# Routed attention and a gated feed-forward on one core: row sums of the first four groups by TensorE in place of GpSimd, their division one turn sooner, weight rounding from turn 0

## The chip, the cores and the metric

The kernel runs on one core of one Trainium2 chip. The metric is the time of one execution in microseconds (us) on the device; the median of 7 runs is given. TensorE (PE) multiplies; its weight loads (PEld) overlap the products. VectorE (DVE), ScalarE (ACT) and GpSimd (POOL) work on whole tiles, each engine in the order in which its instructions were issued. SyncE (SP) issues nearly all DMAs, in order too.

## What is computed

```python
# q, k, v: (4, 8, 768, 64); centroids: (8, 16, 64); all fp32
q_assign = argmax(q_n @ c_n.T)              # nearest of 16 centroids, per head
k_assign = argmax(k_n @ c_n.T)
mask   = q_assign[:, :, :, None] == k_assign[:, :, None, :]
scores = where(mask, q @ k.T / 8, -1e9)
attn   = softmax(scores)                    # along the keys
x      = (attn @ v), heads side by side     # (3072, 512)
h      = x @ w_in                           # (512, 2048)
out    = (h * sigmoid(1.702 * h)) @ w_out   # (2048, 512)
```

`w_in` and `w_out` arrive as 64-bit floats and are rounded to fp32 on the chip.

## The kernel before

**Units, groups, turns.** Two heads make a pair `p` (16 pairs, four per batch; `HP` is 4). A group `g` is one pair with one half (384) of its queries; the first four groups (g below `HP`) are the first half of the first batch, the next four its second half. A group has six units, one per tile of 128 keys (`kt` 0 to 5). Scores are held transposed: 128 keys on the partitions, 384 queries of each of the two heads along the free dimension. The main loop (L551 on) takes two units per turn, so a group lasts three turns (`TG`), a batch 24 (`TB`), and there are 96 turns and two more to drain.

**One turn, in the order issued.** `scores` (L384, PE) writes two PSUM tiles `s` of a pool with two buffers. In the first batch `part` (L398, PE) adds a product of one-hot codes to them, which makes pairs of query and key with different centroids hugely negative; `exps` (L409, ACT) takes the exponential. In later batches the mask is a multiplication on DVE instead (L420). `mask` also adds up the row sums: for each unit with `kt` above 0 POOL adds the 128x768 tile `A` into `sum` (L430), five adds per group. `values` (L441, PE) handles the units of the turn before: for each of the two heads one product of 64 columns of `v` with `A`, accumulated over the six units in a PSUM tile `o`; after the last unit ACT copies `o` to `x` (L446).

**Division.** `normalise(g)` runs in turn 3g+4. It multiplies `sum` by a tile of ones (L453, PE, two products), which adds up the 128 partitions and spreads the result over 64 rows; DVE takes the reciprocal (L456) and multiplies `x` by it (L458). In the first half of the first batch it stands behind the turn's preparation, later ahead of it. `check` (L468, L470, ACT) then takes statistics of the reciprocal.

**Preparation of pairs.** `PREP` has seven steps: four `prep_turn` (three transposes on PE, L262, then a copy on ACT, L267), `prep_near` (products with the centroids, L276, copy L282), `prep_assign` (transposes L287, then four or five DVE instructions, L293 to L308, which find the nearest centroid) and `prep_hot` (twelve transposes, L349, evacuated by DVE, L354, and ACT, L356), or for later pairs `prep_spread`. All these, the products of the division and the feed-forward part share PSUM tiles from one pool, `ps_m`, with three buffers (`bank()`). `prep(p, 0)` loads `v` of its pair, and steps 1 and 3 load the next `q` or `k`. Assignments of the pairs 1 to 4 fall in the turns 1, 3, 6 and 9, `prep_hot` of pairs 1 to 3 in the turns 2, 4 and 7.

**Weights.** 32 chunks of 128x512, 512 KB each as read. `load_w` issues a DMA on SP into one of three `raw` buffers. `split_w` has two DVE instructions (L159, L161), then two on ACT (L163, L165); `join_w` three on DVE (L171, L174, L177). `round_next` loads chunk i+2, splits chunk i and joins chunk i-1, which frees the buffer that the load needs. Before, it is called once in the turns 1, 2, 4, 5, 6, 8, 9 and 10, and from turn 12 on two or three times per turn. The feed-forward part calls `round_to` to force what it needs.

**Feed-forward.** After every fourth group `normalise` appends 28 pieces: 16 of `first` (four products of `w_in` with `x`, L487, tanh on ACT, L492, gate on DVE, L494) and 12 of `second` (four products each with `w_out`, L504). `rate` spreads them over the turns: `owed` grows by it in every turn that begins with pieces left. The pieces stand at the end of a turn.

Of the kernel before, what the change touches and what calls it, by code (L numbers as in the profile page):

```python
# [38 lines left out]
def fast(  # L39
# [21 lines left out]
    nc = tc.nc  # L61

    B, H, S, D = q.shape
# [3 lines left out]
    NJ = S // P  # L67
    HALF = S // 2
    NH = NJ // 2
    HP = H // 2  # L70
    NPAIR = B * HP
    NCH = DM // P
    NF = DF // P
# [24 lines left out]
    def bank():  # L98
        return ps_m.tile([P, 512], FP32, name="m")

    def short():
        return tmp.tile([P, HALF], FP32, name="short")
# [4 lines left out]
    def load_qk(p, w):  # L107
        t = inp.tile([P, NJ, 2, D], FP32, name="in")
        b, hp = divmod(p, HP)
        for a in range(2):  # L110
            nc.sync.dma_start(
                out=t[:, :, a, :],
                in_=(q, k)[w][b, 2 * hp + a].rearrange("(p j) d -> p j d",
                                                       j=NJ))
        qk_in[p, w] = t

    def load_v(p):
        b, hp = divmod(p, HP)
        t = pairs.tile([P, 2, NJ, D], FP32, name="inv")
        nc.sync.dma_start(  # L120
            out=t.rearrange("p a j d -> p a (j d)"),
            in_=v[b, 2 * hp:2 * hp + 2].rearrange(
                "a (p j) d -> p a (j d)", j=NJ))
        v_in[p] = t
# [18 lines left out]
    def load_w(i):  # L143
        if i < NW:
            t = wp.tile([P, WN, 2], I32, name="raw")
            nc.sync.dma_start(out=t.rearrange("p n t -> p (n t)"),
                              in_=w_chunks[i][1])
            w_raw[i] = t
# [5 lines left out]
    def split_w(i):  # L154

        hi = w_raw[i][:, :, 1]
        w = w_chunks[i][0]
        e = wp.tile([P, WN], I32, name="e")
        nc.vector.tensor_scalar(out=e, in0=hi, scalar1=EXP, scalar2=None,  # L159
                                op0=ALU.bitwise_and)  # L160
        nc.vector.tensor_scalar(out=w.bitcast(I32), in0=hi, scalar1=0xFFFFF,  # L161
                                scalar2=None, op0=ALU.bitwise_and)
        nc.scalar.activation(out=e, in_=e, func=AF.Relu, scale=8.0,  # L163
                             bias=low[:, 0:1])
        nc.scalar.activation(out=w, in_=w.bitcast(I32), func=AF.Copy,  # L165
                             scale=2.0 ** -20, bias=1.0)
        w_pow[i] = e

    def join_w(i):
        raw, e, w = w_raw.pop(i), w_pow.pop(i), w_chunks[i][0]  # L170
        nc.vector.scalar_tensor_tensor(  # L171
            out=e, in0=raw[:, :, 1], scalar=-2 ** 31, in1=e,
            op0=ALU.bitwise_and, op1=ALU.bitwise_or)
        nc.vector.scalar_tensor_tensor(  # L174
            out=w, in0=raw.bitcast(U32)[:, :, 0], scalar=2.0 ** -52, in1=w,
            op0=ALU.mult, op1=ALU.add)
        nc.vector.tensor_tensor(out=w, in0=w, in1=e.bitcast(FP32),  # L177
                                op=ALU.mult)
# [3 lines left out]
    def round_next():  # L182
        i = w_done[0]
        if i < NW:
            load_w(i + 2)
            split_w(i)
        if 0 < i <= NW:
            join_w(i - 1)
        w_done[0] += 1

    def round_to(n):
        while w_done[0] <= min(n, NW):
            round_next()

    load_qk(1, 0)
    load_v(0)


# [10 lines left out]
    ones = const.tile([P, D], FP32, name="ones")  # L209
# [34 lines left out]
    for a in range(2):  # L244
        rows = slice(a * D, (a + 1) * D)
        nc.vector.tensor_copy(
            out=cT[rows, :, a, :],
# [120 lines left out]

    NG = 2 * NPAIR
    NU = NG * NJ  # L370
    s_of, A_of, sum_of, o_of, O_of, xT_of = {}, {}, {}, {}, {}, {}

    def split(g):
        b, r = divmod(g, 2 * HP)
        h, hp = divmod(r, HP)
        return b * HP + hp, h

    def scores(u):
        g, kt = divmod(u, NJ)
        p, h = split(g)  # L380
        ps = ps_s.tile([P, 2, 512], FP32, name="s")
        for a in range(2):
            rows = slice(a * D, (a + 1) * D)
            nc.tensor.matmul(out=ps[:, a, 0:HALF],  # L384
                             lhsT=T[p, 1][rows, kt * P:(kt + 1) * P],
                             rhs=T[p, 0][rows, h * HALF:(h + 1) * HALF],
                             start=True, stop=(p >= HP))
        s_of[u] = ps[:, :, 0:HALF]
# [22 lines left out]

    def mask(u):

        g, kt = divmod(u, NJ)
        p, h = split(g)
        s = s_of.pop(u)
        if p >= HP:
            A_of[u] = ap.tile([P, 2, HALF], FP32, name="A")
            for a in range(2):
                nc.vector.scalar_tensor_tensor(  # L420
                    out=A_of[u][:, a, :],
                    in0=qcode[p][:, a, h * HALF:(h + 1) * HALF],
                    scalar=code[p][:, kt % NH, 1, kt // NH, a:a + 1],
                    in1=s[:, a, :], op0=ALU.is_equal, op1=ALU.mult)
        A = A_of[u]
        if kt == 0:
            return
        if kt == 1:
            sum_of[g] = ap.tile([P, 2, HALF], FP32, name="sum", bufs=2)
        nc.gpsimd.tensor_tensor(out=sum_of[g],  # L430
                                in0=A_of[u - 1] if kt == 1 else sum_of[g],
                                in1=A, op=ALU.add)

    def values(u):
        g, kt = divmod(u, NJ)
        p, h = split(g)
        if kt == 0:
            o_of[g] = ps_o.tile([P, 512], FP32, name="o")
        A = A_of.pop(u)
        for a in range(2):  # L440
            nc.tensor.matmul(out=o_of[g][a * D:(a + 1) * D, 0:HALF],  # L441
                             lhsT=v_in[p][:, a, kt, :], rhs=A[:, a, :],
                             start=(kt == 0), stop=(kt == NJ - 1))
        if kt == NJ - 1:
            O_of[g] = xp.tile([P, HALF], FP32, name="x")
            nc.scalar.copy(O_of[g], o_of.pop(g)[:, 0:HALF])  # L446

    def normalise(g):

        sm = sum_of.pop(g)  # L450
        ps = bank()
        for a in range(2):
            nc.tensor.matmul(out=ps[a * D:(a + 1) * D, 0:HALF], lhsT=ones,  # L453
                             rhs=sm[:, a, :], start=True, stop=True)
        rec = recs[g] = short()
        nc.vector.reciprocal(out=rec, in_=ps[:, 0:HALF])  # L456
        x = xT_of[g] = O_of.pop(g)
        nc.vector.tensor_tensor(out=x, in0=x, in1=rec, op=ALU.mult)  # L458
        if g % HP == HP - 1:
            ffn.extend(ffn_chunks(g // HP))  # L460
# [14 lines left out]
    ffn = deque()  # L475
# [47 lines left out]
    TG = NJ // 2  # L523
    TB = 2 * HP * TG

    prep_at = {}
    for p in range(1, NPAIR):
        b, hp = divmod(p, HP)
        for i in range(2 if p == 1 else 0, len(PREP)):
            if p == 1:  # L530
                t = (i - 2) // 2
            elif b == 0:
                t = (hp - 2) * TG + 1 + i // 2
            else:
                t = b * TB + (-20, -8, -2, 1)[hp] + i
# [5 lines left out]
    def prep(p, i):  # L541
        if i == 0 and p:
            load_v(p)
        PREP[i](p)
        if i in (1, 3) and loads:
            load_qk(*loads.popleft())

    rate = (NF + NH * (NF // 4)) / (TB / 2 - 0.5)
    owed = 0.0
    for p, i in [(0, i) for i in range(6)] + [(1, i) for i in range(2)]:  # L550
        prep(p, i)  # L551
        if p == 0 and i in (1, 3):
            load_w(i // 2)
    for t in range(NT + 2):
        us = range(2 * t, 2 * t + 2) if t < NT else ()
        for u in us:
            scores(u)
        if t == 0:
            prep(0, 6)
        for u in us:  # L560
            part(u)
        for u in us:
            exps(u)
        second = t >= TB // 2
        if second:
            round_next()
        for u in us:
            mask(u)
        work = sorted(prep_at.get(t, ()), key=lambda w: PREP[w[1]] != prep_near)
        while work and PREP[work[0][1]] == prep_near:  # L570
            prep(*work.pop(0))
        if 1 <= t <= NT:
            for u in range(2 * t - 2, 2 * t):
                values(u)
        owed = owed + rate if ffn else 0.0
        g = (t - 2) // TG if t >= 2 and (t - 2) % TG == TG - 1 else None
        if g is not None and second:
            normalise(g)
        for p, i in work:
            prep(p, i)  # L580
        if g is not None and not second:
            normalise(g)
        if recs:
            check(*recs)
        if second or t and t % 4 != 3:
            round_next()
        while owed >= 1 and ffn:
            ffn.popleft()()
            owed -= 1
        if second and t % 2:  # L590
            round_next()


    ok = const.tile([P, 2, 2 * NPAIR], FP32, name="ok")
# [6 lines left out]
    ps = bank()  # L601
# [451 lines left out]
```

## Time and profile before

| what | value |
|---|---|
| median of 7 runs | 1088.79 us |
| lowest and highest | 1086.58 and 1089.24 us |
| the profiled execution's own time | 1086.99 us |
| its span, first to last instruction | 1085.2 us |
| mean granted TensorE clock | 0.989 |
| POOL L430, 160 adds | 294.2 us busy, 1839 ns each |
| first score product; first `w_in` product | 11.80 us; 93.65 us |

The page of the profile gives each engine's busy time and share, then the span in 40 slices of 27.1 us, one digit each: the busy share in tenths, and for PEclk the clock that was granted. A row of the stretches gives the limits and the length of the stretch, then for PE, PEld, DVE, ACT and POOL the busy us with the number of instructions, the granted clock, the share of the DMA engines and GB/s. A row of a timeline gives the start, the length (from the first start to the last end), engine, line, operation, output, inputs, shapes and count, and in brackets the idle time of the engine before it with what ended it. An fp32 product appears as two records on PE, so a turn's four `values` products are eight records.

### The profile page before, as it was taken

The numbers are of one execution on the slowest core, as the hardware profiler recorded it, in microseconds if no ns is written. First come the engines' busy times: TensorE is split into PE (matmuls) and PEld (weight loads), VectorE is DVE, ScalarE is ACT, GpSimd is POOL, SyncE is SP. The second block draws the span as 40 slices with busy tenths as digits, with TensorE's granted clock in tenths as the row PEclk, the third lists the DMA queues.
The fourth block names the chain that finished last, engine by engine and source line by source line (L and its number), as shares of the span: only waits on it lengthen the run. The fifth ranks groups of instructions, "written<-read, shape, count | busy, mean of one in ns | idle before, by whom it ended". The sixth has DMA issues, their size and how long they took to land. (4 is left out here: it accounts for less than half of the span.)

```text
span 1085.2 us, 10456 instructions
## 1 busy us (share of the span) xinstructions
PE 1048.2 (97%) x3982; PEld 492.7 (45%) x3982; DVE 491.2 (45%) x744; ACT 354.5 (33%) x665; POOL 295.4 (27%) x168
## 2 busy tenths in 40 slices
PE   7878799999999999999999999999999999999997
PEld 4323354445544455445554455444554445444543
DVE  3889999135442444424453164423552244431200
ACT  4664555233322333223432233223332133311100
POOL 2654232213222333122231142222232333230000
PEclk9998899999999999999999999999999999999999
DMA  8533453111100010102200000010000000000000
GB/s 216 149 95 102 132 148 94 47 49 26 41 22 27 10 30 15 31 25 54 51 23 17 20 16 15 15 56 24 8 9 10 10 10 1 1 10 20 1 11 22
DMA packets 64812, 45.13 MB, mean 42 GB/s; under 512 B 51952, under 2 KB 57584, under 8 KB 64752
## 3 DMA queue, kind: packets, MB, share of 16 engines
q1 hardware_dynamic: 64608, 44.33, 14.3%
q8 instruction: 33, 0.54, 0.2%
q14 instruction: 27, 0.22, 0.1%
q10 hardware_dynamic: 144, 0.03, 0.0%
HBM read 38.04 MB, written 6.31 MB: 41 GB/s over the span
## 5 line engine op out<-in xcount | busy, mean ns | idle before, releaser
L430 POOL TENSOR_TENSOR sum<-sum,A 128x768 f32<-128x768 f32 x128 | 235.4, 1839 | 460.6 <-DVE A L420 364.2
L487 PE MATMUL m<-x,w_in 128*128 128x384 f32 x1024 | 348.4, 495 | 10.0 <-ACT T L267 4.4
L504 PE MATMUL m<-w_out,g 128*128 128x512 f32 x768 | 337.8, 594 | 0.7 <-ACT short L282 0.7
L420 DVE SCALAR_TENSOR_TENSOR A<-qb,code,s 128x384 f32<-128x384 uint8 x288 | 157.6, 610 | 274.7 <-ACT s L409 251.9
L487 PEld LDWEIGHTS m<-x,w_in 128*128 128x128 f32 x1024 | 193.0, 193 | 150.5 <-issue 18.2
L504 PEld LDWEIGHTS m<-w_out,g 128*128 128x128 f32 x768 | 143.3, 190 | 175.6 <-issue 171.5
L494 DVE SCALAR_TENSOR_TENSOR g<-g,m 128x384 f32<-128x384 f32 x128 | 70.0, 553 | 219.8 <-ACT g L492 219.8
L384 PE MATMUL s<-T,T 64*128 64x384 f32 x768 | 151.5, 513 | 8.2 <-ACT A L409 8.2
L409 ACT ACTIVATE s<-s 128x768 f32<-128x768 f32 x144 | 107.9, 793 | 136.1 <-PE s L384 136.1
L441 PE MATMUL o<-A,inv 128*64 128x384 f32 x768 | 145.8, 501 | 0.0
L492 ACT ACTIVATE g<-m 128x384 f32<-128x384 f32 x128 | 61.5, 486 | 196.1 <-PE m L487 195.9
L430 POOL TENSOR_TENSOR sum<-A 128x768 f32<-128x768 f32 x32 | 58.8, 1838 | 215.6 <-DVE A L420 179.5
L384 PEld LDWEIGHTS s<-T,T 64*128 64x128 f32 x768 | 66.0, 187 | 91.6 <-issue 51.4
L456 DVE RECIPROCAL short<-m 128x384 f32<-128x384 f32 x32 | 81.7, 2552 | 25.8 <-PE m L453 25.8
L441 PEld LDWEIGHTS o<-A,inv 128*64 128x64 f32 x768 | 46.8, 137 | 84.7 <-issue 84.4
L510 ACT ACTIVATE y<-m 128x512 f32<-128x512 f32 x24 | 14.3, 594 | 155.9 <-PE m L504 142.7
L468 ACT ACTIVATE short<-short 128x384 f32<-128x384 f32 x32 | 16.7, 523 | 109.5 <-DVE x L458 109.5
L409 ACT ACTIVATE A<-s 128x768 f32<-128x768 f32 x48 | 36.1, 804 | 20.2 <-PE s L398 20.2
L267 ACT COPY T<-m 128x384 f32<-128x384 f32 x64 | 29.7, 479 | 37.0 <-PE m L262 36.9
L262 PE MATMUL m<-ident,in 128*128 128x128 f32 x192 | 33.7, 296 | 3.0 <-ACT T L267 1.7
L163 ACT ACTIVATE e<-e,low 128x512 int32<-128x512 int32 x32 | 23.1, 723 | 30.8 <-DVE e L159 30.6
L262 PEld LDWEIGHTS m<-ident,in 128*128 128x128 f32 x192 | 21.4, 146 | 22.1 <-issue 11.1
(68 smaller groups left out, 373.9 us busy)
## 6 DMA issues: line engine op xcount, KB each, us to landing
raw<-in_moe_w_in_dram SPq DMA_DIRECT2D x16, 512.0 KB
raw<-in_moe_w_out_dram SPq DMA_DIRECT2D x16, 512.0 KB
in<-in_q_dram SPq DMA_DIRECT2D x32, 192.0 KB
in<-in_k_dram SPq DMA_DIRECT2D x32, 192.0 KB
inv<-in_v_dram SPq DMA_DIRECT2D x16, 384.0 KB
out_dram<-y SPq DMA_DIRECT2D x24, 256.0 KB
qb<-line SPq DMA_DIRECT2D x12, 192.0 KB
line<-row SPq DMA_DIRECT2D x12, 1.5 KB
```

Source lines behind the costliest of these rows:

```text
L262: nc.tensor.transpose(out=ps[:, n * P:(n + 1) * P], in_=qk_in[p, w][:, h * NH + n].rearrange("p a d -> p (a d)"), identity=ident)
L267: nc.scalar.copy(dst, ps[:, 0:HALF])
L384: nc.tensor.matmul(out=ps[:, a, 0:HALF], lhsT=T[p, 1][rows, kt * P:(kt + 1) * P], rhs=T[p, 0][rows, h * HALF:(h + 1) * HALF], start=True, ...
L409: nc.scalar.activation(out=A_of[u] if p < HP else s, in_=s, func=AF.Exp, scale=SCALE)
L420: nc.vector.scalar_tensor_tensor(out=A_of[u][:, a, :], in0=qcode[p][:, a, h * HALF:(h + 1) * HALF], scalar=code[p][:, kt % NH, 1, kt // NH ...
L430: nc.gpsimd.tensor_tensor(out=sum_of[g], in0=A_of[u - 1] if kt == 1 else sum_of[g], in1=A, op=ALU.add)
L441: nc.tensor.matmul(out=o_of[g][a * D:(a + 1) * D, 0:HALF], lhsT=v_in[p][:, a, kt, :], rhs=A[:, a, :], start=(kt == 0), stop=(kt == NJ - 1))
L456: nc.vector.reciprocal(out=rec, in_=ps[:, 0:HALF])
L487: nc.tensor.matmul(out=ps[:, 0:HALF], lhsT=w_in[:, c, f * P:(f + 1) * P], rhs=xT[c], start=(c == 0), stop=(c == NCH - 1))
L492: nc.scalar.activation(out=g, in_=ps[:, 0:HALF], func=AF.Tanh, scale=0.851)
L494: nc.vector.scalar_tensor_tensor(out=g, in0=g, scalar=1.0, in1=ps[:, 0:HALF], op0=ALU.add, op1=ALU.mult)
L504: nc.tensor.matmul(out=ps[:, 0:DM], lhsT=hs[f][:, n * P:(n + 1) * P], rhs=w_out[:, f, :], start=(f == 0), stop=(f == NF - 1))
```

## The change

For the first four groups the row sums come from PE: next to each `values` product stands one of `ones` with the same `A`, accumulated over the six units in a PSUM tile `D_of[g]` taken from `ps_m` at the group's first unit. POOL adds nothing for these groups, and `normalise` reads `D_of[g]` directly, without products of its own. Their division comes in turn 3g+3 instead of 3g+4, ahead of the turn's preparation. The first two weight loads are issued before and after the load of pair 1's `q`; one `round_next` stands ahead of the assignment of pair 0, one in the middle of turn 0, and one at the end of every turn; from turn 12 on there are two per turn. The feed-forward pieces of the first half are spread over one turn more.

```diff
+    load_w(0)
     load_qk(1, 0)
+    load_w(1)
     load_v(0)
...
     def mask(u):
...
-        if kt == 0:
+        if kt == 0 or g < HP:
             return
...
     def values(u):
...
+        if g < HP:
+            if kt == 0:
+                D_of[g] = bank()
+            for a in range(2):
+                nc.tensor.matmul(out=D_of[g][a * D:(a + 1) * D, 0:HALF],
+                                 lhsT=ones, rhs=A[:, a, :], start=(kt == 0),
+                                 stop=(kt == NJ - 1))
...
     def normalise(g):
-        sm = sum_of.pop(g)
-        ps = bank()
-        for a in range(2):
-            nc.tensor.matmul(out=ps[a * D:(a + 1) * D, 0:HALF], lhsT=ones,
-                             rhs=sm[:, a, :], start=True, stop=True)
+        if g < HP:
+            ps = D_of.pop(g)
+        else:
+            sm = sum_of.pop(g)
+            ps = bank()
+            for a in range(2):
+                nc.tensor.matmul(out=ps[a * D:(a + 1) * D, 0:HALF], lhsT=ones,
+                                 rhs=sm[:, a, :], start=True, stop=True)
...
-    rate = (NF + NH * (NF // 4)) / (TB / 2 - 0.5)
+    norm_at = {TG * g + (TG if g < HP else TG + 1): g for g in range(NG)}
     owed = 0.0
     for p, i in [(0, i) for i in range(6)] + [(1, i) for i in range(2)]:
+        if (p, i) == (0, 5):
+            round_next()
         prep(p, i)
-        if p == 0 and i in (1, 3):
-            load_w(i // 2)
...
         second = t >= TB // 2
-        if second:
+        if second or t == 0:
             round_next()
...
-        owed = owed + rate if ffn else 0.0
-        g = (t - 2) // TG if t >= 2 and (t - 2) % TG == TG - 1 else None
-        if g is not None and second:
-            normalise(g)
+        if not ffn:
+            owed = 0.0
+        else:
+            owed += (NF + NH * (NF // 4)) / (TB / 2 - 0.5 + (t < TB + 1))
+        if t in norm_at:
+            normalise(norm_at[t])
         for p, i in work:
             prep(p, i)
-        if g is not None and not second:
-            normalise(g)
         if recs:
             check(*recs)
-        if second or t and t % 4 != 3:
-            round_next()
+        round_next()
         while owed >= 1 and ffn:
             ffn.popleft()()
             owed -= 1
-        if second and t % 2:
-            round_next()
```

More of the change, by code (lines that the diff above doesn't have):

```diff
@@ L370, in fast @@
     NU = NG * NJ
-    s_of, A_of, sum_of, o_of, O_of, xT_of = {}, {}, {}, {}, {}, {}
+    s_of, A_of, sum_of, o_of, D_of, O_of, xT_of = {}, {}, {}, {}, {}, {}, {}
     def split(g):
```

## The prediction

> **What bounds the kernel now.** I read the busy shares first, then the 40 slices, then stretches of the span, then the timelines of the engines.
>
> ```profile
> span 1085.2 us, 10456 instructions
> PE 1048.2 (97%) x3982; PEld 492.7 (45%) x3982; DVE 491.2 (45%) x744; ACT 354.5 (33%) x665; POOL 295.4 (27%) x168
> ...
> PE   7878799999999999999999999999999999999997
> ...
> DVE  3889999135442444424453164423552244431200
> ...
> PEclk9998899999999999999999999999999999999999
> ```
>
> Over the whole span PE is the bound. Only its first five slices (136 us) are below nine tenths, and there DVE has nines and the granted clock eights. So whatever the change gains must come out of that stretch, and any PE work it adds is paid in full unless it falls into a hole there. The same stretch cut at the start of turn 0, of turn 12 and of turn 17:
>
> ```profile
> 11.80:80.44 68.64, 56.34 (x380) 24.73 (x380) 50.97 (x75) 42.21 (x80) 34.92 (x18) 0.99 0.51 141
> 80.44:136.31 55.87, 46.15 (x168) 20.97 (x168) 54.85 (x69) 28.67 (x52) 19.67 (x10) 0.83 0.39 120
> 136.31:200.00 63.69, 62.67 (x259) 29.56 (x259) 55.60 (x83) 33.41 (x63) 19.01 (x10) 1.00 0.36 108
> ```
>
> After the length come PE, PEld, DVE, ACT and POOL busy, then the clock. PE is idle for 68.64 - 56.34 = 12.3 us in turns 0 to 11 and 55.87 - 46.15 = 9.7 us in turns 12 to 16. In the second stretch the clock of 0.83 costs another 46.15 x 0.17 = 7.8 us. Together 29.8 us can be won back; from turn 17 on PE is full (1.0 us idle). In turns 12 to 16 DVE is busy 54.85 of 55.87 us: DVE is the bound there, and POOL is part of the reason:
>
> ```profile
> 80.53 4.39 POOL L430 TENSOR_TENSOR sum<-sum,A 128x768 f32<-128x768 f32 x2 [3.77 <-ACT A L409]
> ```
> ```profile
> 78.37 0.68 DVE L174 SCALAR_TENSOR_TENSOR w_in<-raw,w_in 128x512 f32<-128x512 uint32 x1
> ...
> 80.96 2.29 DVE L174 SCALAR_TENSOR_TENSOR w_in<-raw,w_in 128x512 f32<-128x512 uint32 x1
> 83.29 2.18 DVE L177 TENSOR_TENSOR w_in<-w_in,e 128x512 f32<-128x512 f32 x1
> ```
> ```profile
> 74.93 1.51 PE L441 MATMUL o<-A,inv 128*64 128x384 f32 x8
> 80.44 2.93 PE L384 MATMUL s<-T,T 64*128 64x384 f32 x8 [4.00 <-ACT A L409]
> ```
>
> The same L174 takes 0.68 us alone and 2.29 us while POOL adds: one of the rounding's instructions is held about 1.6 us per add. PE then waits 4.00 us for the exponentials, which stand on ACT behind the rounding's L163 and L165, and those behind DVE. After the hole L384 takes 2.93 us instead of 1.56: the clock had been halved.
>
> **The change, part by part.**
>
> *Products with ones.* Each of the 24 units of groups 0 to 3 gets two products of the form of L441 (128x64 weights, 384 columns, the two halves of PE's columns in turn). A turn of L441 goes from 41.35 to the next start at 42.80 us, 1.45 us. Twelve turns cost 12 x 1.45 = 17.4 us. The four L453 pairs that go took 0.75 each (120.49 to 121.24), 3.0 us. PE has **14.4 us more to do**. If the added products interleave worse than L441, the bound above is a full-array product like L487 (2.65 us per 8 records, 17.4 x 2.65/1.45 = 31.8 us); below, nothing for a product that falls into a hole. I take 17.4, since shape and alternation are L441's.
>
> *POOL's additions.* Twenty adds of 1.84 us leave. POOL itself bounds nothing. What is saved is about ten holdups on DVE in turns 1 to 13 at 1.6 us, 16 us of DVE; a clean round is 2.60 us (42.69 to 45.29). From turn 12 the second half's adds go on as before, five per three turns.
>
> *Rounding sooner.* Before, 8 rounds are done by the end of turn 11; now 1 ahead of the first assignment, 2 in turn 0, 1 in each of turns 1 to 11: 14. Six rounds, 15.6 us of DVE, leave turns 12 to 21, where two per turn replace two or three. Each round also puts L163 and L165 (0.62 + 0.52 us) on ACT ahead of the next exponentials.
>
> *Loads.* SP issues raw 0 and 1 ahead of pair 1's q and of v 0. At 229 GB/s (the first 20 us) 512 KB take 2.3 us, so q of pair 1 lands 2.3 us later, v 0 and k of pair 1 4.6 us later. Their first uses are at 11.06, 19.79 and 16.21 us, and they were issued at 3.51, 5.23 and 6.39: covered, 0. Uncovered, up to 2.3 us. Later raw loads wait on SP for a round's join, with q and k loads behind them; those run more than two turns ahead. 0.
>
> *Division sooner, and a bank held.* The division of group g moves from turn 3g+4, after that turn's preparation, to turn 3g+3, before it. There it stands on DVE ahead of the assignment (turns 3, 6, 9), which the round follows. The row sums hold one of the three PSUM banks for three turns, so the preparation has two. Let E be the end of the products in turn 3. DVE then does L456 and L458 (2.67 + 0.47 us), five assignment instructions (2.73), split (0.67), join (1.93), then L354 (0.56): bank free at E + 9.1. PE meanwhile has L287 0.4, scores and masks 1.91, values and ones 2.9, a 0.6 wait for the assignment, transposes 0.76: it stands at E + 6.6 and waits for a bank. Two more banks through ACT's L356 and L267 bring the next scores to E + 10.75, against E + 7.4 unblocked: **3.4 us lost in turn 4**. In turn 7, with one transpose group instead of three behind it, the same sum gives 2.7. In turn 10 the way runs over ACT: 3.14 + 2.73 + L159 0.45 + L163 0.62 + L165 0.52 + first exponential 0.85 = E + 8.3, against 5.3 of PE work: 2.9. Turn 0 keeps its 0.67 + 0.90, and turns 1 and 2 lose 1.6 to bank and ACT waits. Turns 0 to 12: **12.2 us**, no less than the 12.3 before, only at other places.
>
> *Turns 13 to 17.* The feed-forward part starts in turn 13 instead of 14, and x of group 3 (division at E + 3.2) arrives before its first product (E + 3.35), so the 2.81 us wait at 98.66 goes. DVE per turn has two rounds 5.2, adds' holdups 5/3 x 1.6 = 2.7, 2.24 gates x 0.5 = 1.1, division 1.0: 10.0 us. PE has 3.35 + 2.24 x 2.65 + 0.5 = 9.8. Nearly even, so short bank waits stay: 0.7 in turn 15, 3.4 in turn 16, 0.6 in turn 17 (the same place as the 4.14 us wait at 128.51). **4.7 us**. Bounds: 0 if DVE keeps ahead, 9.7 as before.
>
> *Sum.* 14.4 + 12.2 + 4.7 - 29.8 = **+1.5 us** on the profiled execution (1086.99 us, 1.8 over its span). The median is 1.8 above that execution, so 1088.79 + 1.5 = 1090.3 us. Break-even is a loss of 15.4 us where I find 16.9.
>
> *The clock.* Holes of 2.77 us and more halved it, the hole of 2.05 us at 46.05 did not, nor did the 3.5 us between 54.85 and 58.32 that hold only transposes and 1.36 us of waiting. My holes are 2.1 to 2.4 us, and transposes stand beside them, so I charge nothing. One drop costs 1.6 to 2.5 us.
>
> The Trainium skill (TensorE: Matmul & The Clock Gate, Part 4: PE-mode transpose) says that transposes do not count as busy for the clock in the way products do, and its Part 1 gives a window of about 3.4 us. The stretch from 54.85 speaks against taking that literally. By the page, turn 4 (5.5 us with transposes alone) and turn 7 (3.8 us) would each drop the clock, and the sum would be some 4 us higher, an estimate.
>
> **Rivals.**
>
> *DVE freed, holes filled.* DVE's 16 us of holdups and six early rounds leave so much slack that turns 13 to 17 lose nothing and the division turns only half of what I charge: 14.4 + 7.7 - 29.8 = -7.7 us, 1081. For it: DVE's 54.85 of 55.87. Against: in turns 3, 6 and 9 the chain is one of order, not of load.
>
> *The clock falls in the division turns.* Holes in turns 4, 7 and 10 grow past about 2.8 us, as at 98.66, and PE runs at half speed after each: 3 x 2.0 on top, +7.5 us, 1096. It decides once DVE's L354 comes later than E + 9.5. For it: holes within 0.5 us of that size. Against: the stretch from 54.85.
>
> *No effect of the adds' absence.* If DVE's long instructions had another cause than POOL, turns 1 to 11 would still be held up; the chain of turn 3 would grow by 1.6, towards 1095. The coincidence of each 2 us instruction with an add speaks against it.
>
> **How the numbers follow.** Near even, 1086 to 1094: 0.45. Freed, below 1086: 0.33. Clock or longer chain, above 1094: 0.22. The predicted time is 1090. A measurement here tells 0.2%, 2.2 us, from no change; of the near-even case 0.27 lie inside and 0.18 above, so faster 0.33, same 0.27, slower 0.40. As both signs weigh, the near-even case's own range is 1086 to 1094; the range that leaves two in ten out is 1080 to 1096.
>
> **What would show it.** Added products near 0.72 us per unit; no DVE rounding over 0.7 us before turn 12; PE waits of 2 us in turns 4, 7 and 10, named by DVE's L354 or ACT's exponentials; first w_in product near 101 us; clock 1.0 up to there. A start of w_in below 96 us makes me wrong on the fast side; a clock below 0.95 before turn 12 on the slow side.

## The result, and the profile after

The changed kernel takes 1091.77 us (median of 13 runs, 1090.15 to 1094.05); the kernel before, run beside it, 1088.68 us. The ratio is 1.0034 with a 95% interval of 1.0026 to 1.0041: slower by 0.3%, 3.1 us by the medians. The prediction was 1090 us, in a range of 1080 to 1096. The profiled execution took 1092.73 us, 5.7 us above the one of before. That is more than the medians differ by, since the first stood 1.0 above its median and the second 1.7 below the 1088.68 of before; the stages below add up to the difference of the spans, 5.6 us.

The page of the changed kernel, the lines that answer to those of before (busy time and share, then tenths of 40 slices):

```profile
span 1090.8 us, 10566 instructions
PE 1059.3 (97%) x4062; PEld 497.3 (46%) x4062; DVE 477.2 (44%) x744; ACT 355.6 (33%) x665; POOL 257.5 (24%) x148
...
PE   7888989999999999999999999999999999999997
...
DVE  4757999124443354414453163423552344431200
```

POOL has lost its 20 adds (37.9 us) and DVE 14.0 us with the same 744 instructions: that is the time for which the adds had held it up. PE has 80 records more (96 for the products with ones, less the 16 of the four divisions). Apart from the last slice, still five slices are below nine tenths, and the sum of the first six has hardly risen (46 before, 48 after).

The stretches of the changed kernel, cut at the start of turns 0, 12, 17 and 22 (limits, length, busy PE, PEld, DVE, ACT and POOL, clock, DMA share, GB/s):

```profile
13.18:96.75 83.57, 73.03 (x457) 31.82 (x456) 55.33 (x97) 50.00 (x89) 0.00 (x0) 0.96 0.48 139
96.75:144.67 47.92, 41.84 (x182) 19.09 (x180) 42.78 (x56) 23.00 (x42) 15.54 (x8) 1.00 0.40 124
144.67:200.41 55.74, 54.98 (x221) 25.86 (x220) 44.76 (x67) 26.93 (x52) 16.25 (x8) 1.00 0.29 88
```

| stage | before | after | difference |
|---|---|---|---|
| up to turn 0 | 11.80 us | 13.18 us | +1.4 |
| turns 0 to 11 | 68.64 us, PE idle 12.3, clock 0.99 | 83.57 us, idle 10.5, clock 0.96 | +14.9 |
| turns 12 to 16 | 55.87 us, idle 9.7, clock 0.83 | 47.92 us, idle 6.1, clock 1.00 | -8.0 |
| from turn 17 on | 948.9 us | 946.1 us | -2.8 |

By the start of turn 17 the changed kernel has one feed-forward piece more behind it, 2.65 us, which the last row gives back. So turns 12 to 16 give 10.6 us and turns 0 to 11 take 14.9. In the first stretch PE waits almost as long as before, at other places. PE's timeline in turn 4, from the last products with ones to the scores of turn 5, and at the end of turn 7:

```profile
43.16 0.81 PE L451 MATMUL m<-A,ones 128*64 128x384 f32 x4
44.80 0.86 PE L351 MATMUL m<-ident_h,hot 128*64 128x128 bf16 x12 [0.83 <-DVE hot L310]
47.87 1.84 PE L264 MATMUL m<-ident,in 128*128 128x128 f32 x9 [2.21 <-DVE qb L356]
49.64 2.93 PE L386 MATMUL s<-T,T 64*128 64x384 f32 x8
...
71.95 0.55 PE L264 MATMUL m<-ident,in 128*128 128x128 f32 x3 [2.34 <-DVE qb L356]
72.43 2.31 PE L386 MATMUL s<-T,T 64*128 64x384 f32 x8
```

The bracket names the instruction whose end let PE go on: DVE's copy out of the bank that the next transposes need. After both holes the scores take 2.93 and 2.31 us instead of 1.56: the clock was halved (granted clock 0.50 from 49.64 to 52.51 us and 0.61 from 72.43 to 75.42). And DVE's and SP's timelines around turn 12:

```profile
102.46 0.43 DVE L159 TENSOR_SCALAR e<-raw 128x512 int32<-128x512 int32 x1 [4.69 <-DMA raw<-in_moe_w_in_dram]
```
```profile
92.85 0.38 SPq L332 DMA_DIRECT2D line<-row  x1
96.63 0.34 SPq L334 DMA_DIRECT2D qb<-line  x1
97.06 0.85 SPq L146 DMA_DIRECT2D raw<-in_moe_w_in_dram  x2
```

SP issued pair 4's `line` at 92.85, stood until it had landed to issue `qb` from it at 96.63, and only then issued weight chunk 14. DVE idled 4.69 us for it, and the division of group 3, on which the feed-forward part waits, stands behind it.

### The profile page after: what moved, and what is told of

It is laid out like the page before. It is cut to its first block, busy times and chain, and to the rows that moved or that the text cites. A ratio compares the mean times of both kernels' runs of the same rounds, so it can differ in the third digit from the quotient of the medians.

```text
span 1090.8 us, 10566 instructions
## 1 busy us (share of the span) xinstructions
PE 1059.3 (97%) x4062; PEld 497.3 (46%) x4062; DVE 477.2 (44%) x744; ACT 355.6 (33%) x665; POOL 257.5 (24%) x148
## 5 line engine op out<-in xcount | busy, mean ns | idle before, releaser
L500 PE MATMUL m<-x,w_in 128*128 128x384 f32 x1024 | 343.3, 489 | 5.0 <-DVE g L507 2.7
L433 POOL TENSOR_TENSOR sum<-sum,A 128x768 f32<-128x768 f32 x112 | 204.8, 1828 | 425.2 <-DVE A L423 361.9
L500 PEld LDWEIGHTS m<-x,w_in 128*128 128x128 f32 x1024 | 190.1, 190 | 143.5 <-issue 12.3
L433 POOL TENSOR_TENSOR sum<-A 128x768 f32<-128x768 f32 x28 | 51.3, 1834 | 294.4 <-DVE A L423 177.9
```

What stands on the lines that cost most here:

```text
L433: nc.gpsimd.tensor_tensor(out=sum_of[g], in0=A_of[u - 1] if kt == 1 else sum_of[g], in1=A, op=ALU.add)
L500: nc.tensor.matmul(out=ps[:, 0:HALF], lhsT=w_in[:, c, f * P:(f + 1) * P], rhs=xT[c], start=(c == 0), stop=(c == NCH - 1))
```

## The experiments

Times are medians. Each ratio is taken against runs of the kernel before on the same chip (1087.6 to 1088.1 us).

**Row sums back on POOL, earlier rounding kept (a_pool_sums).**

```diff
-        if kt == 0 or g < HP:
+        if kt == 0:
...
-        if g < HP:
+        if g < 0:
...
-    norm_at = {TG * g + (TG if g < HP else TG + 1): g for g in range(NG)}
+    norm_at = {TG * g + (TG + 1): g for g in range(NG)}
...
```

The lines left out put the division of these groups behind the preparation again and the pieces back to their old pace.

> Row sums of groups 0 to 3 back on POOL and their division back in turn 3g+4 behind the preparation; only the earlier rounding and loads of the change stay. Theory: the products with ones are the cost (14.4 us of PE) and the earlier rounding alone is a gain in turns 12 to 16, partly paid back in turns 0 to 11, where DVE goes from 51 busy of 68.6 us to about 67 and is still held up by adds. Expected 1086 us (1083 to 1090), with DVE instructions of 2.2 us back before turn 12. Rival (the earlier rounding and loads are what costs, the sums are neutral): 1091 us or more.

1089.39 us, ratio 1.0011 (1.0002 to 1.0020): between the two, and the expected gain isn't there. DVE is held up in turns 1 to 12 as before (an L174 of 2.32 us at 52.13, of 2.31 at 71.00, of 2.30 at 88.76), now with six more rounds to do, and PE has waits of 1.86, 1.37, 1.38, 2.38 and 3.99 us up to the start of turn 12, for DVE's copies or for exponentials. The earlier rounding alone moves the shortage forward, it doesn't remove it. By the ratio it costs 1.2 us (0.2 to 2.2), so it isn't all of the 3.1 us either.

**Row sums on PE, rounding and loads as before (b_sums_alone).**

```diff
-    load_w(0)
...
-        round_next()
+        if second or t and t % 4 != 3:
+            round_next()
...
+        if second and t % 2:
+            round_next()
```

> Products with ones and the earlier division stay; rounding and loads are as in the kernel before (8 rounds by the end of turn 11, none in turns 3 and 7). Theory: 15.6 us of DVE come back into turns 12 to 21, where DVE is the bound, while turn 4 loses less because no round stands in turn 3. Expected 1095 us (1091 to 1100), DVE full in turns 12 to 16 with clock drops there. Rival (the rounding's place is worth nothing): 1091.8 us, within 1 us.

1096.97 us, ratio 1.0077 (1.0061 to 1.0094), as expected: with the sums on PE the kernel is 9 us above the one before without the earlier rounding, and 3 with it. Here turn 3 happens to have no round, and the 2.21 us wait of turn 4 is 0.31 us. Turn 6 has one, and the wait of turn 7 is the same 2.34 us as in the changed kernel, but this time the scores behind it run at full clock:

```profile
66.47 0.55 PE L262 MATMUL m<-ident,in 128*128 128x128 f32 x3 [2.34 <-DVE qb L354]
66.94 1.56 PE L384 MATMUL s<-T,T 64*128 64x384 f32 x8
```

**No rounding in the division turns (c_round_off).**

```diff
-        round_next()
+        for _ in range(1 if second or t in (0, 11) else t % TG):
+            round_next()
```

> As the changed kernel, but no rounding in turns 3, 6 and 9 (two rounds in turns 2, 5 and 8 instead), so that the copy that frees a bank and the exponentials no longer stand behind split and join. Theory (the holes of turns 4, 7 and 10 are an order of instructions on DVE, 2.6 us too late, and bring the clock down): the waits of 2.2, 2.3 and 2.1 us fall below 1 us, the clock stays at 1.0 before turn 12, expected 1085 us (1082 to 1088). Rival (the holes come from DVE's load or from the held bank alone): 1091 us, within 1.5 us.

1081.22 us, ratio 0.9931 (0.9919 to 0.9943): 10.5 us below the changed kernel with the same instructions in another order, and 3.8 us below what I had expected. The same places on PE's timeline:

```profile
44.45 0.86 PE L351 MATMUL m<-ident_h,hot 128*64 128x128 bf16 x12 [0.82 <-DVE hot L310]
45.62 1.66 PE L264 MATMUL m<-ident,in 128*128 128x128 f32 x9 [0.31 <-DVE qb L356]
47.21 1.56 PE L386 MATMUL s<-T,T 64*128 64x384 f32 x8
...
66.09 0.55 PE L264 MATMUL m<-ident,in 128*128 128x128 f32 x3 [0.32 <-DVE qb L356]
```

The waits of 2.21 and 2.34 us are 0.31 and 0.32, the third, 2.08 us in turn 10, is gone, and the scores run at full clock. The bank is still held and DVE has the same load: what made the holes was that the copy and the exponentials stood behind split and join.

**Few products with ones (g_few_ones), and the same without rounding in the division turns (h_round_off_few_ones).**

```diff
             if kt == 0:
                 D_of[g] = bank()
-            for a in range(2):
+            for a in range(2 if kt in (0, NJ - 1) else 0):
```

> As the changed kernel, but products with ones only for the first and the last key tile of each of groups 0 to 3 (16 of 24 units' products left out, so the row sums of these groups are incomplete); the bank is held as long, DVE and ACT do the same. Prices the products: theory says they lie on PE's path, 16 x 0.72 = 11.6 us, expected 1080 us (1078 to 1084). Rival (they fall into PE's holes): 1088 us or more.

> No rounding in turns 3, 6 and 9, and products with ones only for the first and last key tile of each of groups 0 to 3 (the row sums of these groups are incomplete). Prices the products once the holes are gone. Theory (16 of 24 units' products came to 5.5 us instead of 11.6 with the holes there, because a hole that is a chain from the end of the sums grew as PE came sooner, and the clock fell three times): now 8 to 11.6 us below the version with all products (1081.2), 1071 us (1069 to 1074). Rival (half of the products' time is hidden whatever the holes): 1076 us or more.

The first took 1086.22 us, ratio 0.9987 (0.9977 to 0.9997), 5.5 us below the changed kernel; the second 1076.44 us, ratio 0.9904 (0.9889 to 0.9919), 4.8 us below c_round_off. I had expected 11.6 and then 8 to 11.6. By the ratios, each against the kernel before on its own chip, it is 5.1 and 2.9 us. So leaving a product out gives back roughly a quarter to a half of its time on PE, with the holes or without; the expectation's reason for the first miss can't be the whole one, since it doesn't hold for the second. PE's timeline of h_round_off_few_ones shows where some 3 us of the rest go:

```profile
40.43 0.86 PE L351 MATMUL m<-ident_h,hot 128*64 128x128 bf16 x12 [1.26 <-DVE hot L310]
54.34 0.55 PE L289 MATMUL m<-ident,short 128*128 128x128 f32 x3 [1.34 <-ACT short L284]
75.91 0.22 PE L325 MATMUL m<-ident_h,qc 128*12 128x128 bf16 x1 [1.68 <-DVE qc L318]
```

In turns 4 and 10 PE comes sooner to what DVE's division and assignment have to deliver (0.82 and 0.44 us in c_round_off), and in turn 6 it waits 1.34 us for ACT where it didn't. A product that fills such a wait costs next to nothing.

**qb's load a turn later (e_line_first), and both orders mended (j_round_off_line).**

```diff
+        def spread():
+            nc.sync.dma_start(
...
+        late.append(spread)
+        if p > HP:
+            late.pop()()
...
         round_next()
+        if t == 11:
+            late.pop()()
```

> As the changed kernel, but the second of pair 4's two small loads (qb from line, which stands on SP until line has landed) is issued at the end of turn 11 instead of turn 10, so that the load of weight chunk 14 no longer stands behind it. Theory (the wait of 4.7 us of DVE for that chunk at 102 us is SP's order, and costs PE about 1.7 us in turn 13 and part of the bank waits of turns 14 to 16): the wait falls below 2.5 us, expected 1089.5 us (1088 to 1091). Rival (the wait is the transfer itself, or DVE has slack there): 1091.8 us, within 1 us.

> Both orders mended: no rounding in turns 3, 6 and 9, and qb's load of pair 4 one turn later on SP. Theory: 1 to 2 us below the version with the first alone (1081.2): 1079.5 us (1078 to 1081). Rival (the chunk's wait is hidden): 1081 us, within 0.7 us.

e_line_first: 1090.63 us, ratio 1.0024 (1.0013 to 1.0036). The interval overlaps that of the changed kernel, so the time alone doesn't decide. The waits of its DVE between 80 and 140 us do:

```profile
DVE e L159 <- DMA raw<-in_moe_w_in_dram: 0.7, 2, 0.4
```

The columns are total, times and longest: 0.7 us instead of 4.7. PE's waits of 1.19 us (turn 13) and 1.76 us (turn 14) are gone with it. j_round_off_line: 1079.69 us, ratio 0.9930 (0.9917 to 0.9944), within its expectation; against c_round_off 1.5 us less by the medians, but only 0.1 by the ratios, with overlapping intervals again. That the wait was SP's order is shown; that removing it is worth the 1 us that the medians give is not clear of the noise.

**POOL's sums with the other round order (i_pool_round_off).** The edits of a_pool_sums and of c_round_off together.

> Row sums on POOL and division in turn 3g+4 as in the kernel before, earlier rounding and loads as in the changed one, and no rounding in turns 3, 6 and 9 (two in 2, 5 and 8). Theory (the adds' holdups on DVE, some 16 us before turn 12, are what the products buy off; the order alone can't): 1087 us (1084 to 1090). Rival (the order of rounding is all, and the products only cost): 14.4 us less PE work than with them, below 1076 us.

1097.48 us, ratio 1.0098 (1.0082 to 1.0113): the rival is out, but I was 10 us too low. DVE's, ACT's and PE's timelines in turn 6:

```profile
53.19 2.30 DVE L174 SCALAR_TENSOR_TENSOR w_in<-raw,w_in 128x512 f32<-128x512 uint32 x1
55.53 2.19 DVE L177 TENSOR_TENSOR w_in<-w_in,e 128x512 f32<-128x512 f32 x1
```
```profile
58.09 0.72 ACT L163 ACTIVATE e<-e,low 128x512 int32<-128x512 int32 x1 [2.50 <-DVE e L159]
...
60.62 0.48 ACT L284 COPY short<-m 128x384 f32<-128x384 f32 x1
```
```profile
61.15 0.90 PE L289 MATMUL m<-ident,short 128*128 128x128 f32 x3 [4.21 <-ACT short L284]
```

With adds on POOL the first of the two rounds has L174 and L177 held up (2.30 and 2.19 us), the second round's split waits for that, ACT waits 2.50 us for the split, and behind it stand the exponentials and the copy that PE needs: 4.21 us. The order that saves 10.5 us with the sums on PE costs 8 us with them on POOL.

**Division behind the assignment (d_division_last).**

```diff
-        if t in norm_at:
+        if t in norm_at and second:
             normalise(norm_at[t])
         for p, i in work:
             prep(p, i)
+        if t in norm_at and not second:
+            normalise(norm_at[t])
```

> As the changed kernel, but in turns 3, 6 and 9 the division stands behind the assignment on DVE instead of ahead of it (still a turn sooner than in the kernel before). Theory: the chain to the round's split and to the bank's release has the same length, 3.1 + 2.7 us, only the 0.8, 0.5 and 0.4 us waits for the assignment go, and the exponentials come 0.8 us later because the statistics on ACT wait for the division: 1091.5 us (1090 to 1093). Rival (the division ahead of the assignment is what makes the holes): 1086 us or less.

1095.95 us, ratio 1.0071 (1.0058 to 1.0085), 4 us above the changed kernel where I had expected none. The waits for the assignment are gone, as expected; the waits behind them grew by more. PE's timeline in turn 4:

```profile
47.71 0.90 PE L264 MATMUL m<-ident,in 128*128 128x128 f32 x3 [3.23 <-DVE qb L356]
49.26 1.54 PE L264 MATMUL m<-ident,in 128*128 128x128 f32 x6 [0.64 <-ACT qb L358]
50.73 2.93 PE L386 MATMUL s<-T,T 64*128 64x384 f32 x8
```

The hole of turn 4 is 3.23 us instead of 2.21, that of turn 7 3.36 us instead of 2.34, that of turn 10 3.96 us instead of 2.08, where the exponentials stand behind the statistics on ACT; and after all three the scores are slow (2.93, 2.63 and 2.93 us). Theory and rival were both wrong here.

**One round in turn 16 (k_no_round_16).** On top of j_round_off_line:

```diff
-        if second or t == 0:
+        if second and t != 16 or t == 0:
             round_next()
```

> Both orders mended (no rounding in turns 3, 6, 9; qb's load later), and turn 16 has one round instead of two, at its end, so that neither the division of group 4 nor the copy of pair 5's turned tile stands behind a round there. Theory: the waits of 0.9 and 1.9 us of turn 16 go and nothing is forced later, 1077 us (1075.5 to 1079). Rival (POOL's adds hold the same instructions up elsewhere): 1079.7 us, within 1 us.

1075.55 us, ratio 0.9887 (0.9872 to 0.9902). This is the best version, 12.1 us below the kernel before on the same chip (1087.61). j_round_off_line and this one, PE's timeline at the same piece of turn 16:

```profile
128.15 4.54 PE L507 MATMUL m<-x,w_in 128*128 128x384 f32 x8 [1.90 <-ACT T L269]
```
```profile
124.28 5.43 PE L507 MATMUL m<-x,w_in 128*128 128x384 f32 x16
```

The 1.90 us wait for ACT's copy goes, and with it the slow clock behind it (4.54 us for eight records that take 2.7).

**The last two mendings without the products (m_pool_mended, n_before_mended).** a_pool_sums, and the kernel before, with qb's load later and one round fewer in turn 16.

> Row sums on POOL and division in turn 3g+4 as before, earlier rounding and loads as in the changed kernel (1089.4 us in that form), with the two mendings that don't touch the division turns: qb's load of pair 4 a turn later, one round in turn 16. Theory (the products with ones are needed, since adds hold DVE up in turns 1 to 11): 1085.5 us (1083.5 to 1088). Rival (the mendings are all of the gain and the products none of it): 1078 us or less.

> The kernel before with the same two mendings alone (qb's load of pair 4 a turn later, one round fewer in turn 16). Theory: the wait of 4.14 us in turn 16 goes with its clock drop, but a round is pushed back into turns where DVE is full: 1085 us (1082.5 to 1088). Rival: 1078 us or less, so that the change isn't needed for the best version.

m_pool_mended 1086.36 us, ratio 0.9983 (0.9974 to 0.9992), as expected. n_before_mended 1081.36 us, ratio 0.9942 (0.9928 to 0.9955), more than expected: the hole of 4.14 us at 128.51 is gone with its slow clock, and PE has no wait in its place. So 6.7 of the 12.1 us (against 1088.07 on its chip) don't need the change at all. The rest, 5.8 us from 1081.36 to 1075.55, takes the products and the earlier rounding with the division turns kept free of rounds; no run has the products with the rounding as before and both mendings, so what each of the two is worth there stays open.

## Why the prediction was right, and what in it was not

The direction and the main reason were right: the products with ones cost somewhat more than the waits won back, because the holes of turns 4, 7 and 10 took the place of the old ones. Slower was given a chance of 0.40 against 0.33 for faster. The size came within 1.8 us, partly by luck: on the two profiled executions, for which the sum was made, it was +1.5 us against a measured +5.7, and the errors below partly cancel. By the prediction's own terms:

- **Products, 17.4 - 3.0 us.** Mis-sized by a little: a turn with ones takes 2.73 us of products (21.93 to 24.66) instead of 1.44, so twelve turns cost 15.5 us instead of 17.4. Charging them in full was right in this sum, since the holes were worked out, and measured, with the products in place. What the sum doesn't tell is what leaving products out would save: 2.9 to 5.5 us for 16 units of some 0.65 us each, because the waits grow.
- **POOL's additions.** Right. No rounding instruction before turn 12 is above 0.73 us, and putting the adds back (a_pool_sums, i_pool_round_off) brings 2.2 us and more back. DVE got 14.0 us back, 16 were predicted.
- **Division and bank.** Right, place by place: waits of 0.6 and 2.5 us were worked out for turn 4 (measured 0.83 and 2.21), 2.7 for turn 7 (0.50 + 2.34), 2.9 for turn 10 (0.44 + 2.08). The bank was to be free 9.1 us after the products of turn 3; it was after 9.0 (38.84 to 47.81). Turns 0 to 12 were to lose 12.2 us; PE's waits over 0.2 us there are 10.4. c_round_off shows the cause: round ahead of copy.
- **Clock.** This term failed. It was charged with nothing, because in the kernel before neither the hole of 2.05 us at 46.05 nor "the 3.5 us between 54.85 and 58.32 that hold only transposes and 1.36 us of waiting" had lowered the clock. The second is misread: its last row is the division's products.

```profile
54.85 0.83 PE L349 MATMUL m<-ident_h,hot 128*64 128x128 bf16 x12
55.62 0.55 PE L262 MATMUL m<-ident,in 128*128 128x128 f32 x3
57.52 0.87 PE L453 MATMUL m<-sum,ones 128*64 128x384 f32 x4 [1.36 <-DVE qb L354]
```

Only 2.5 us there are without products, from 55.02 to 57.52, and 3.2 us ahead of the scores at 46.05; neither speaks against a drop after longer stretches. In the changed kernel 5.7 us without products (43.97 to 49.64) and 4.2 us (68.25 to 72.43) were followed by half clock, at 1.6 us each (2.93 and 2.31 us for 1.56, and the rows around them), and 2.75 us in turn 10 were not. The Trainium skill's rule (TensorE: Matmul & The Clock Gate, Part 4: PE-mode transpose) that transposes don't keep the clock up the way products do agrees with turns 4 and 7 of this trace, where only transposes and waits stand between 43.97 and 49.64 us and between 68.25 and 72.43. But the same 4.2 us of turn 7 left the clock full in b_sums_alone, and the 2.08 us wait of turn 10, at full clock here (1.61 us of scores behind it), was followed by slow scores in e_line_first (2.39 us). So which holes lower the clock differs between executions. Waits alone can do it: in the kernel before, the wait of 2.77 us at 112.76 stood between products, and the eight records behind it took 4.54 us. What transposes add to that no run here shows. The prediction's other reading of that page, some 4 us more, was nearer to this profile's 3.2 us.

- **Turns 13 to 17, 4.7 us.** Measured 1.19 + 1.76 + 0.20 + 0.93 + 1.89 + 0.76 = 6.7. The waits that were foreseen, in turns 15 to 17, came to 3.8 us; those of 1.19 and 1.76 in turns 13 and 14 were not foreseen. The term that failed is that of the loads: "Later raw loads wait on SP for a round's join, with q and k loads behind them; those run more than two turns ahead. 0." It asked what stands behind the raw loads, and not what stands ahead of them: pair 4's two small loads, of which the second waits for the first. That is the 4.69 us wait at 102.46, and e_line_first took it away. The first `w_in` product came at 106.02 us instead of near 101.
- **Start, 0.** Turn 0 began 1.4 us later in this execution, and its scores took 2.48 us instead of 1.56. Neither is fixed: with the same loads turn 0 began between 11.23 and 13.42 us in the other profiles, with waits for pair 0's k of 0 to 1.44 us, and its scores took 1.56 us.

So the sum was short by 3.2 us of clock, 2.0 of turns 13 to 17, 1.4 ahead of turn 0 and 0.9 in it, and long by 1.9 of products and 1.8 in turns 0 to 12: 5.3 us where the spans differ by 5.6. The rival *the clock falls in the division turns* came half true: its condition, holes past 2.8 us, didn't come, and the clock fell in two of the three turns all the same. *DVE freed, holes filled* is what another order made of the kernel in c_round_off: 1081.22 us, where that rival had been given 1081.

## What to carry to other kernels

When a change frees an engine, ask which instruction of it the bound engine waits for, and what stands ahead of that one in the queue: the same instructions in another order were worth 10.5 us here, while the 14 us of DVE freed without that order did not even pay for the products. When work is added to or taken from the bound engine, work its waits out again: 16 of 24 units' products gave back about half of their time or less. Before a hole is called harmless, check row by row what stands in it; before a load is called covered, read the queue ahead of it as well as behind it. And try the small mendings on the kernel before too: more than half of the gain of the best version needed none of the change.

## What the runs showed of the hardware

An add on POOL of 1.84 us holds up one rounding instruction on DVE, 2.0 to 2.3 us instead of 0.42 to 0.69 (before, 80.96 to 91.58 us), while a reciprocal that started with two adds stayed at 2.55 us (before, 73.12) and the multiplication behind it took 1.39 us instead of 0.56.

The clock can fall after holes on PE of some 2 us, but the length of a hole doesn't settle it. A hole of the same length at the same place was followed by a lower clock in one execution and not in another:

| hole on PE | clock full behind it | clock lowered behind it |
|---|---|---|
| 2.0 us, end of turn 5 | before: scores 1.62 us, clock 1.00 | n_before_mended: 2.82 us, 0.53 |
| 2.34 us, end of turn 7 | b_sums_alone: scores 1.56 us, clock 1.00 | changed kernel: 2.31 us, 0.61 |
| 2.08 us, end of turn 10 | changed kernel: scores 1.61 us, clock 1.00 | e_line_first: 2.39 us, 0.62 |
| 1.9 us, turn 16 | changed kernel: piece of `first` 2.85 us, clock 1.00 | j_round_off_line: 4.54 us, 0.62 |

The clock is the mean granted one over that row or the few behind it. So a hole of some 2 us can cost 1 to 2 us more than its length, and one execution's profile doesn't tell whether it will.
